# Attention outputs turned in 32x32 blocks by VectorE, with w_in's rows to match: a local-global attention followed by a hardswish MLP

## The chip, the cores and the metric

The kernel runs on one core of one Trainium2 chip. The metric is device time in microseconds; three runs of the kernel before the change have a median of 340.51 us (339.76 to 341.34).

## The reference

Eight batches of attention with 8 heads of 64. Each batch has 512 local tokens, which attend to a band of 32 tokens to each side and to the 32 global tokens, and 32 global tokens, which attend to everything. All 4352 rows then pass an MLP of 512 to 2048 to 512 with a hardswish between.

```python
s_g = scale * np.matmul(q_g, k_all.transpose(0, 1, 3, 2))
out_g = np.matmul(sm(s_g), v_all)
s_ll = np.where(np.abs(pos[:, None] - pos[None, :]) <= 32, scale * np.matmul(q_l, k_l.transpose(0, 1, 3, 2)), -1e9)
s_l = np.concatenate([scale * np.matmul(q_l, k_g.transpose(0, 1, 3, 2)), s_ll], axis=-1)
out_l = np.matmul(sm(s_l), np.concatenate([v_g, v_l], axis=2))
x = np.concatenate([out_g, out_l], axis=2).transpose(0, 2, 1, 3).reshape(B * S, H * D)
h = x @ w_in
return (h * np.clip(h + 3.0, 0.0, 6.0) / 6.0) @ w_out
```

## The kernel before

Everything runs in fp16 with fp32 sums. A planner (`Plan`) writes one static order for all engines: operations stand in named streams, each with engine, cost, dependencies and the buffers that it takes, and `lay` picks, again and again, the operation that can start first, ranked by stream among those that start at nearly the same time. Low ranks go first. `SWITCH` is what the planner charges PE for going between tile shapes, `ALONE` and `SPARE` are its thresholds for a single group of small tiles and for giving an eviction to VectorE (DVE) rather than ScalarE (ACT).

Attention of a batch has four local pairs (`local`, two 32-token blocks from each half of the batch) and two global groups (`globe`, four heads each). A pair goes through these stages:

- `s`: products of q and k in small tiles into PSUM banks `s` (batch 0 partly into `m`), 64 matmuls in batches 0 and 1 and 32 later;
- `mx`: DVE adds the mask and takes the maximum, eight times (line 664); `ex`: ACT exponentiates, eight times (line 670);
- `t`: eight PE transposes into bank `t` (line 679); `etc`: the result is copied to SBUF as `et`, by ACT or DVE (lines 308 and 310, the helper `either`);
- `av`: 32 PE matmuls with V into the banks `a` (line 693); `nm`: DVE takes reciprocals and multiplies (lines 701 and 702), which gives `x`, 128 x 512 in fp16;
- `xp`: four PE transposes of 128 x 128 through bank `t` (line 715); `xpc`: a copy to `xt` by ACT or DVE.

The two global groups do the same with maxima over two banks, `top` (lines 751 and 752), five transposes (line 768), products with V of their own (line 777), normals (lines 785 and 786), and one transpose for both at the end (line 792), which fills `xg`.

The MLP's first half (`first`, line 821) takes `xt` against `w_in` for 16 units `c` of 128 hidden columns, four matmuls each, into one of three banks `m`; ACT makes the clipped part `t1` (line 833) and DVE the product `gts` (the gate, line 828). Batch 0 is done in two halves of 256 tokens, the other batches in one of 512. The second half (`second`, line 850) takes `gts` against `w_out`, 16 matmuls of 512 columns for a tile of 128 rows, copies the sum to `ot` (lines 858 and 860), and SP's queue stores it. The global rows of all batches go through the MLP together at the end (`moe_global`), and one last local tile after them is done in two column halves. The planner lays MLP work of earlier batches between the attention of later ones.

All DMAs are issued at line 298: loads with a cast to fp16 on POOL's queue, on SP's queue the stores and the copies inside SBUF (`rawq`, `rawk`, `gn`, `vs` from `vg`). q and k of batches 2 to 7 are turned by DVE in 32 x 32 blocks (lines 571, 575, 578). POOL also shifts V into strips (line 486).

`xt` holds hidden row d of heads in an order that `load_w_in` matches, since its DMAs put the rows of `w_in` in the same order on the 128 partitions.

## Time and profile before

| | |
|---|---|
| median of three runs | 340.51 us (339.76 to 341.34) |
| the profiled execution's own time | 340.96 us |
| its span on the core | 339.2 us |
| PE, DVE, ACT busy | 313.6, 257.0, 234.1 us |
| mean granted clock of PE | 0.983 |
| instructions on PE (matmuls), DVE, ACT, POOL | 4456, 952, 576, 195 |

The span runs from the first to the last instruction in the trace; the execution's own time has what lies around it as well. The profile's groups name line, engine, operation, output and input, count, busy time, mean time of one and the idle time before them with what ended it. Its timeline gives start and length of runs of equal instructions. PE's lengths include the time that a matmul spends in the array, so that neighbours overlap.

### The profile page before, as it was taken

The numbers are of one execution on the slowest core, as the hardware profiler recorded it, in microseconds if no ns is written. First come the engines' busy times: TensorE is split into PE (matmuls) and PEld (weight loads), VectorE is DVE, ScalarE is ACT, GpSimd is POOL, SyncE is SP. The second block draws the span as 40 slices with busy tenths as digits, with TensorE's granted clock in tenths as the row PEclk, the third lists the DMA queues.
The fourth block names the chain that finished last, engine by engine and source line by source line (L and its number), as shares of the span: only waits on it lengthen the run. The fifth ranks groups of instructions, "written<-read, shape, count | busy, mean of one in ns | idle before, by whom it ended". The sixth has DMA issues, their size and how long they took to land.

```text
span 339.2 us, 11248 instructions
## 1 busy us (share of the span) xinstructions
PE 313.6 (92%) x4456; PEld 169.5 (50%) x4456; DVE 257.0 (76%) x952; ACT 234.1 (69%) x576; POOL 156.2 (46%) x195
## 2 busy tenths in 40 slices
PE   0648879899999999999999999999999999999996
PEld 0536656454455455544554555454545544445654
DVE  5887997678988799989998999899969844433310
ACT  4778778555888697679867784799699644443431
POOL 8899589108961982694359258756000000000000
PEclk9976999999999999999999999999999999999999
DMA  8989999979960996999679948991000000010103
GB/s 131 185 154 165 185 227 164 177 204 147 221 124 35 154 206 86 91 153 179 145 99 150 169 90 80 183 174 41 31 33 34 35 32 33 31 60 34 62 34 92
DMA packets 107076, 39.27 MB, mean 116 GB/s; under 512 B 92368, under 2 KB 100816, under 8 KB 107024
## 3 DMA queue, kind: packets, MB, share of 16 engines
q0 software_dynamic: 93536, 17.44, 64.6%
q1 hardware_dynamic: 12912, 20.99, 22.7%
q8 instruction: 35, 0.57, 0.7%
q10 hardware_dynamic: 576, 0.13, 0.2%
q14 instruction: 17, 0.14, 0.1%
HBM read 35.39 MB, written 8.91 MB: 131 GB/s over the span
## 4 chain that ended last, share of the span: by engine, by line
PE 87%; DVE 7%; issue 2%; POOL 1%; ACT 1%; POOLq 0%; ACTq 0%
PE m L850 36%; PE m L821 33%; PE t L679 5%; PE a L693 3%; PE s L624 2%; PE t L715 2%; DVE gts L828 1%; PE t L768 1%; PE s L735 1%; PE s L637 1%; PE a L777 1%; DVE sm L664 1%; POOL wout L298 1%; DVE kt L534 1%; DVE qt L529 1%
## 5 line engine op out<-in xcount | busy, mean ns | idle before, releaser
L850 PE MATMUL m<-wout,gts 128*128 128x512 f16 (+1 forms) x560 | 135.1, 373 | 0.0
L828 DVE SCALAR_TENSOR_TENSOR gts<-t,m 128x512 f16<-128x512 f32 (+1 forms) x160 | 95.2, 602 | 46.1 <-ACT t L833 45.0
L821 PE MATMUL m<-xt,win 128*128 128x512 f16 (+1 forms) x576 | 126.9, 359 | 3.0 <-DVE gts L828 1.9
L833 ACT ACTIVATE t<-m 128x512 f32<-128x512 f32 (+1 forms) x160 | 84.3, 532 | 44.6 <-PE m L821 41.2
L486 POOL COPY vs<-v 32x1056 f32<-32x1056 f32 (+3 forms) x81 | 78.2, 966 | 34.9 <-DMA v<-in_v_l_dram 30.1
L670 ACT ACTIVATE ex<-sm,mx 128x128 f16<-128x128 f32 x256 | 86.1, 394 | 8.4 <-DVE mx L664 7.9
L821 PEld LDWEIGHTS <-win 128*128 128x128 f16 x640 | 59.9, 99 | 54.3 <-issue 4.2
L850 PEld LDWEIGHTS <-gts 128*128 128x128 f16 x560 | 51.1, 98 | 48.5 <-issue 0.7
L664 DVE CUSTOM_DVE_ANT_0 sm<-s,mask 128x128 f32<-128x128 f32 x240 | 56.9, 285 | 5.9 <-PE s L624 2.9
L858 ACT COPY ot<-m 128x512 f32<-128x512 f32 (+1 forms) x34 | 19.5, 573 | 16.9 <-PE m L850 16.2
L298 POOL DMA_DIRECT2D rawq<-in_q_l_dram x12 | 12.6, 1057 | 36.2 <-DMA vs<-vg 16.3
L298 POOL DMA_DIRECT2D v<-in_v_l_dram x32 | 28.2, 905 | 0.0
L702 DVE TENSOR_TENSOR x<-a,rec 128x512 f16<-128x512 f32 x32 | 22.1, 692 | 1.1
L664 DVE DVE_READ_ACCUMULATOR2_ANT mx<- 128x1 f32 x256 | 21.3, 83 | 0.0
L679 PE MATMUL t<-ident,ex 128*128 128x128 f16 x256 | 20.9, 228 | 0.0
L679 PEld LDWEIGHTS <-ex 128*128 128x128 f16 x256 | 17.2, 102 | 5.5 <-issue 0.7
L637 PE MATMUL s<-kt,qt 32*32 32x128 f16 x384 | 7.0, 246 | 12.3 <-DVE kt L542 10.0
L571 DVE STREAM_TRANSPOSE qt<-rawq 128x512 f16<-128x512 f16 x24 | 15.9, 692 | 0.0
L575 DVE STREAM_TRANSPOSE kt<-rawk 128x512 f16<-128x512 f16 x24 | 15.8, 687 | 0.0
L308 ACT COPY et<-t 128x1024 f16<-128x1024 f16 x13 | 13.1, 1010 | 3.5 <-PE t L679 3.4
L637 PEld LDWEIGHTS <-qt 32*32 32x32 f16 x512 | 6.5, 102 | 17.7 <-issue 9.6
L310 DVE COPY et<-t 128x1024 f16<-128x1024 f16 x19 | 13.0, 685 | 3.0 <-PE a L693 2.6
(95 smaller groups left out, 262.7 us busy)
## 6 DMA issues: line engine op xcount, KB each, us to landing
out_dram<-ot SPq DMA_DIRECT2D x31, 256.0 KB, 2.1
vs<-vg SPq DMA_DIRECT2D x32, 132.0 KB, 5.8
v<-in_v_l_dram POOLq DMA_DIRECT2D x32, 128.0 KB, 6.5
rawq<-in_q_l_dram POOLq DMA_DIRECT2D x12, 256.0 KB, 5.8
rawk<-in_k_l_dram POOLq DMA_DIRECT2D x12, 256.0 KB, 7.2
rawq<-rawq SPq DMA_DIRECT2D x12, 254.0 KB, 5.6
rawk<-rawk SPq DMA_DIRECT2D x12, 254.0 KB, 5.7
win<-in_moe_w_in_dram POOLq DMA_DIRECT2D x8, 256.0 KB, 6.2
```

The lines of the kernel that those rows point to most:

```text
L298: eng.dma_start(out=o() if callable(o) else o, in_=i() if callable(i) else i)
L486: (nc.gpsimd if op.engine == "POOL" else nc.vector).tensor_copy(out=o(), in_=i())
L637: nc.tensor.matmul(out=scored(r)[quarter(e ^ r, f), z:z + P], lhsT=pairs(qt[k.slot])[rows, c, i * W:(i + 1) * W, bb], rhs=pairs(kt[k.slot] ...
L664: nc.vector.tensor_tensor_reduce(out=sms[sm.slot], in0=scored(c // 2)[:, z:z + P], in1=masks[:, m, :], scale=-scale, scalar=3.0e38, op0=AL ...
L670: nc.scalar.activation(out=exs[ex.slot][:, un, c, :], in_=sms[sm.slot], func=EXP, scale=-1.0, bias=mxs[mx.slot])
L679: nc.tensor.matmul(out=turned(tp)[:, z:z + P], lhsT=exs[ex.slot][:, un, c, :], rhs=ident, is_transpose=True)
L702: nc.vector.tensor_tensor(out=xs[x.slot], in0=o[:, :, :, 0:D], in1=recs[rec.slot].to_broadcast([P, 2, NC, D]), op=ALU.mult)
L821: nc.tensor.matmul(out=o if len(x.shape) == 2 else o.rearrange("p (a c) -> p a c", a=2), lhsT=w_in_t[c // 8][:, m, (c % 8) * P:(c % 8 + 1) ...
L828: nc.vector.scalar_tensor_tensor(out=g, in0=shape(t1s[t1.slot][:, 0:n]), scalar=1.0, in1=shape(mps[ps.slot][:, 0:n]), op0=ALU.min, op1=ALU ...
L833: r = plan.add("t1", Op(("ACT", 0.09 + n * 0.00083), lambda: nc.scalar.activation(out=t1s[t1.slot][:, 0:n], in_=mps[ps.slot][:, 0:n], func ...
L850: nc.tensor.matmul(out=mps[ps.slot][:, 0:n], lhsT=gfn(c), rhs=w_out_t[c // 4][:, c % 4, cols], start=(c == 0), stop=(c == NDFF - 1))
L858: nc.scalar.copy(out=o, in_=i)
```

## The change

- The four PE transposes of `x` and their copy become one DVE transpose in 32 x 32 blocks from `x` straight to `xt`; those of the global outputs likewise, straight to `xg`. A block transpose moves no data between groups of 32 partitions, so the products with V now write each head to the group of partitions that it needs (`values`), and `w_in`'s rows are loaded in the new order, over 128 partitions in place of 64.
- Tokens lie in `xt` in another order, so each tile of 128 result rows is stored in two halves of 64 rows.
- The two global groups of a batch are joined from their products with V on: `globe` computes scores to `et`, and the new `globe_values` does both groups' products, one normal and one block transpose. Their two score banks are one tile, and one instruction takes the maximum over both.
- In batch 0 and in `moe_global`, two units `c` share a bank `m`, one clipped part and one gate of 512 columns. The buffers `gts` are held in groups of four units (`CG`).
- The planner's ranks and two of its thresholds have other values, so its order differs everywhere.

```diff
-    SWITCH, ALONE = 0.097, 0.0
-    SPARE, PHASES = 0.3, 9
+    SWITCH, ALONE = 0.097, 0.5
+    SPARE, PHASES = 0.6, 9
...
+    PARTS, CG = 2, 4
...
-    for c in range(NDFF):
+    for c in range(NDFF // CG):
...
-    gts = [tiles(f"gts{r}_", NDFF, [P, Sl], FP16) for r in range(2)]
+    gts = [tiles(f"gts{r}_", NDFF // CG, [P, CG, Sl], FP16) for r in range(2)]
...
-    sps = tiles("s", 2, [P, 512], FP32, pp)
+    sps = tiles("s", 1, [P, 2, 512], FP32, pp)[0]
...
-                       ("s", -1), ("mx", lambda n: 1.2 if n < 33 else 2.7), ("ex", 1.2), ("t", -0.5), ("etc", 0), ("av", 0), ("nm", 0),
-                       ("xp", -1.2), ("xpc", 0), ("gx", 1), ("gxc", 1),
-                       ("mf", lambda n: 9 + n * 1e-3), ("ms", lambda n: 9 + (n + 2 * NDFF + 2) * 1e-3), ("t1", 0), ("gate", -1.4), ("ot", 1.5)):
+                       ("s", -1), ("mx", lambda n: 1.2 if n < 33 else 2.7), ("ex", 1.2), ("t", -0.5), ("etc", 0), ("av", -1.5), ("nm", 0),
+                       ("xp", -0.5), ("gx", 1),
+                       ("mf", lambda n: 9 + n * 1e-3), ("ms", lambda n: 9 + (n + PARTS * NDFF + 2) * 1e-3), ("t1", 0.7), ("gate", 0.1), ("ot", 2.2)):
...
-        rows = moe_w_in.rearrange("(k a e d) c -> a k d e c", k=2, a=2, e=2)
+        rows = moe_w_in.rearrange("(k h a d) c -> k a h d c", k=2, h=4, a=2)
         got = []
         for i in range(2):
             for k in range(2):
                 for a in range(2):
-                    got.append(load("l0", "POOL", 0.65, 1.4, w_in_t[i][a * D:(a + 1) * D, 2 * k:2 * k + 2],
-                                    rows[a, k, :, :, i * n:(i + 1) * n], got[-AHEAD:][:1] if len(got) >= AHEAD else ()))
+                    got.append(load("l0", "POOL", 0.65, 1.4, w_in_t[i][:, 2 * k + a], rows[k, a, :, :, i * n:(i + 1) * n],
+                                    got[-AHEAD:][:1] if len(got) >= AHEAD else ()))
...
         def values():
             o = summed(av)
             for un, i in enumerate(pair):
-                for c in range(NC):
-                    for e in range(2):
-                        for f in range(2):
-                            nc.tensor.matmul(out=o[quarter(e, f), un, c, 0:D + 1],
+                for f in range(2):
+                    for kh in range(2):
+                        for hq in range(4):
+                            h = 4 * kh + hq
+                            c, e = h // 2, h % 2
+                            nc.tensor.matmul(out=o[hq * W:(hq + 1) * W, f, 2 * un + kh, 0:D + 1],
                                              lhsT=ets[et.slot][:, un, c, quarter(e, f) if b >= WORDS else quarter(e ^ (c // 2), f)],
-                                             rhs=vs[v.slot][:, i % NU, (i + NI * f) // NU, 2 * c + e, 0:D + 1])
+                                             rhs=vs[v.slot][:, i % NU, (i + NI * f) // NU, h, 0:D + 1])
...
-        xt, xp = st["xt"], Buf(home, 1)
+        xt = st["xt"]
 
         def xturn():
-            o = turned(xp)[:, 0:4 * P].rearrange("d (k z n q) -> d k z n q", k=2, z=NU, n=2)
-            for un in range(2):
-                for kk in range(2):
-                    nc.tensor.matmul(out=o[:, kk, :, un, :], lhsT=xs[x.slot][:, un, 2 * kk:2 * kk + 2].rearrange("p a d -> p (a d)"),
-                                     rhs=ident, is_transpose=True)
-        a = plan.add("xp", Op(("PE", 0.24), xturn, done, [xp], [x], lat=0.25, n=8))
-        st["xT", n] = either(
-            "xpc", 0.5, 0.36,
-            lambda: xts[xt.slot].rearrange("d k (f t) -> d k f t", f=2)[:, :, :, 2 * n * W:(2 * n + 2) * W],
-            lambda: turned(xp)[:, 0:4 * P].rearrange("d (k f t) -> d k f t", k=KC, f=2), [a], new, [xp])
+
+            nc.vector.transpose(out=xts[xt.slot][:, :, n * P:(n + 1) * P].rearrange("p k (t q) -> p t k q", q=W),
+                                in_=xs[x.slot].rearrange("p f (u k) (a q) -> p (f u) (k a) q", u=2, a=2))
+        st["xT", n] = plan.add("xp", Op(("DVE", 0.7), xturn, done, new, [x]))
...
         def top():
-            for f in range(2):
-                nc.vector.tensor_reduce(out=tops[mx.slot][:, f:f + 1], in_=sps[f][:, 0:N1].rearrange("q (a c) -> q a c", a=1), axis=AX, op=ALU.max)
-            nc.vector.tensor_scalar(out=mxs[mx.slot], in0=tops[mx.slot][:, 0:1], scalar1=tops[mx.slot][:, 1:2], scalar2=-scale,
-                                    op0=ALU.max, op1=ALU.mult)
-        t = plan.add("mx", Op(("DVE", 1.0), top, [sc], [mx], ()))
+            nc.vector.tensor_reduce(out=tops[mx.slot][:, 0:1], in_=sps[:, :, 0:N1], axis=AX, op=ALU.max)
+            nc.vector.tensor_scalar(out=mxs[mx.slot], in0=tops[mx.slot][:, 0:1], scalar1=-scale, scalar2=None, op0=ALU.mult)
+        t = plan.add("mx", Op(("DVE", 0.86), top, [sc], [mx], ()))
...
-        def values():
+        def values(av):
             for i in range(NJ + 1):
                 val = v0[v.slot][:, i] if i < NJ else vg[v.slot]
                 for cc, e, z in four:
-                    nc.tensor.matmul(out=aps[av.slot][z, 0, 0:D + 1], lhsT=etgs[et.slot][:, i * P + z.start:i * P + z.stop],
-                                     rhs=val[:, 2 * (2 * cc + s) + e, 0:D + 1], start=(i == 0), stop=(i == NJ))
-        a = plan.add("av", Op(("PE", 0.26), values, [c, st["g4"]] + st["v0"], [av], [et, v], lat=0.3, n=40, mode=("tall", "tall")))
-        if s == 0:
-            st["xgn"] = Buf("xgn", 1)
-        xgn, rec = st["xgn"], Buf("rec", 1)
+                    q = 2 * of(cc) + e
+                    nc.tensor.matmul(out=aps[av.slot][q * W:(q + 1) * W, 0, cc * D1:cc * D1 + D + 1],
+                                     lhsT=etgs[et.slot][:, i * P + z.start:i * P + z.stop],
+                                     rhs=val[:, 4 * cc + q, 0:D + 1], start=(i == 0), stop=(i == NJ))
+        st.setdefault("globe", []).append((values, c, et))
+
+    def globe_values(b):
+
+        st = state[b]
+        both, v = st["globe"], st["v"]
+        av, xgn, rec = Buf("a", 1), Buf("xgn", 1), Buf("rec", 1)
+        a = plan.add("av", Op(("PE", 0.48), lambda: [f(av) for f, _, _ in both], [c for _, c, _ in both] + [st["g4"]] + st["v0"],
+                              [av], [et for _, _, et in both] + [v], lat=0.3, n=80, mode=("tall", "tall")))
 
         def normal():
-            nc.vector.reciprocal(out=recs[rec.slot][:, 0, 0, :], in_=aps[av.slot][:, 0, D:D + 1])
-            nc.vector.tensor_tensor(out=xgns[xgn.slot][:, s, :], in0=aps[av.slot][:, 0, 0:D],
-                                    in1=recs[rec.slot][:, 0, 0, :].to_broadcast([P, D]), op=ALU.mult)
-        n = plan.add("nm", Op(("DVE", 0.36), normal, [a], [rec] + ([xgn] if s == 0 else []), [av, rec]))
-        st.setdefault("gn", []).append(n)
-        if s == 1:
-            tp2 = Buf(home, 1)
-            a = plan.add("gx", Op(("PE", 0.06), lambda: nc.tensor.matmul(
-                out=turned(tp2)[:, 0:P], lhsT=xgns[xgn.slot].rearrange("q s d -> q (s d)"), rhs=ident,
-                is_transpose=True), st["gn"], [tp2], [xgn], lat=0.25, n=2))
-            st["xg"] = either("gxc", 0.25, 0.2, lambda: xg[:, :, b * Sg:(b + 1) * Sg],
-                              lambda: turned(tp2)[:, 0:P].rearrange("d (k g) -> d k g", k=KC), [a], (), [tp2])
+            o = aps[av.slot][:, 0, 0:2 * D1].rearrange("p (k d) -> p k d", k=2)
+            r = recs[rec.slot][:, 0, 0:2, :]
+            nc.vector.reciprocal(out=r, in_=o[:, :, D:D + 1])
+            nc.vector.tensor_tensor(out=xgns[xgn.slot], in0=o[:, :, 0:D], in1=r.to_broadcast([P, 2, D]), op=ALU.mult)
+        n = plan.add("nm", Op(("DVE", 0.45), normal, [a], [rec, xgn], [av, rec]))
+        st["xg"] = plan.add("gx", Op(("DVE", 0.22), lambda: nc.vector.transpose(
+            out=xg[:, :, b * Sg:(b + 1) * Sg], in_=xgns[xgn.slot].rearrange("p k (a q) -> p (k a) q", q=W)), [n], (), [xgn]))
...
-    def first(xfn, n, gfn, deps, takes, reads):
+    def first(xfn, n, cs, gfn, deps, takes, reads):
+
         ps, t1 = Buf("m", 1), Buf("t1", 1)
-        two = lambda t: t if len(t.shape) == 2 else t.rearrange("p a c -> p (a c)")
-
-        def mm(c):
+        all_ = n * len(cs)
+
+        def mm(k, c):
             for m in range(KC):
                 x = xfn(m)
-                o = mps[ps.slot][:, 0:n]
-                nc.tensor.matmul(out=o if len(x.shape) == 2 else o.rearrange("p (a c) -> p a c", a=2),
+                nc.tensor.matmul(out=mps[ps.slot][:, k * n:(k + 1) * n],
                                  lhsT=w_in_t[c // 8][:, m, (c % 8) * P:(c % 8 + 1) * P], rhs=x,
                                  start=(m == 0), stop=(m == KC - 1))
 
...
-        def make(c):
-            a = paced(Op(("PE", 4 * n * 0.000423), lambda: mm(c), deps + w_in_l[c // 8], [ps], reads, lat=0.25, n=8), n / Sl / NDFF)
-            r = plan.add("t1", Op(("ACT", 0.09 + n * 0.00083), lambda: nc.scalar.activation(
-                out=t1s[t1.slot][:, 0:n], in_=mps[ps.slot][:, 0:n], func=RELU, bias=0.5, scale=1.0 / 6.0), [a], [t1], ()))
-            return plan.add("gate", Op(("DVE", 0.07 + n * 0.00104), gate, [r], takes, [ps, t1]))
-        return make
+        a = [paced(Op(("PE", 4 * n * 0.000423 + (0.02 if n < 256 else 0.0)), lambda k=k, c=c: mm(k, c), deps + w_in_l[c // 8], [] if k else [ps], reads, lat=0.25, n=8), n / Sl / NDFF)
+             for k, c in enumerate(cs)]
+        r = plan.add("t1", Op(("ACT", 0.09 + all_ * 0.00083), lambda: nc.scalar.activation(
+            out=t1s[t1.slot][:, 0:all_], in_=mps[ps.slot][:, 0:all_], func=RELU, bias=0.5, scale=1.0 / 6.0), a, [t1], ()))
+        return plan.add("gate", Op(("DVE", 0.2 + all_ * 0.00078), gate, [r], takes, [ps, t1]))
...
-        st["gts"] = [Buf(f"gts{c}", NJ) for c in range(NDFF)]
+        st["gts"] = [Buf(f"gts{c}", CG * NJ) for c in range(NDFF // CG)]
         st["gd"] = {c: [] for c in range(NDFF)}
-        parts = 2 if b == 0 else 1
+        parts = PARTS if b == 0 else 1
         n = HB // parts
+        per = NI // 2 // parts
...
+            for c in range(0, NDFF, parts):
+                cs = range(c, c + parts)
+                g = st["gts"][c // CG]
+
...
+                got = first(lambda m, view=view: view(xts[xt.slot][:, m, :]) if parts > 1 else xts[xt.slot][:, m, :], 2 * n, cs, gated,
+                            deps, [g] if at == 0 and c % CG == 0 else [], [xt])
+                for d in cs:
+                    st["gd"][d].append(got)
 
     def moe_second(b, j, parts=1):
         st = state[b]
-        row = b * S + Sg + j * P
-        second(lambda c: gts[st["gts"][c].slot][c][:, j * P:(j + 1) * P], lambda c: [st["gts"][c]], lambda c: st["gd"][c],
-               [(out[row:row + P, :], 0, P)], parts)
+        rows = out[b * S + Sg:(b + 1) * S].rearrange("(f r) d -> f r d", f=2)
+        second(lambda c: gts[st["gts"][c // CG].slot][c // CG][:, c % CG, j * P:(j + 1) * P], lambda c: [st["gts"][c // CG]], lambda c: st["gd"][c],
+               [(rows[f, j * P // 2:(j + 1) * P // 2], f * P // 2, P // 2) for f in range(2)], parts)
 
...
             for s in range(2):
                 globe(b, s)
+            globe_values(b)
```

51 lines of the change are left out of this document (27 added, 24 removed).

## The prediction

> **What bounds the kernel now.** I read the page first (engine shares, the chain that ended last), then busy time by stretches.
>
> ```profile
> PE 313.6 (92%) x4456; PEld 169.5 (50%) x4456; DVE 257.0 (76%) x952; ACT 234.1 (69%) x576; POOL 156.2 (46%) x195
> PE 87%; DVE 7%; issue 2%; POOL 1%; ACT 1%; POOLq 0%; ACTq 0%
> ...
> 21.00:22.00 1.00, 0.18 (x15) 0.02 (x3) 0.73 (x2) 0.26 (x1) 0.96 (x3) 0.50 0.46 83
> ...
> 28.00:30.00 2.00, 2.00 (x11) 1.39 (x10) 0.61 (x2) 1.62 (x4) 2.00 (x4) 0.50 0.97 167
> ...
> 31.00:32.00 1.00, 1.00 (x12) 0.66 (x8) 0.88 (x3) 0.85 (x3) 1.00 (x3) 1.00 1.09 175
> ...
> 120.00:140.00 20.00, 20.00 (x280) 10.31 (x279) 19.77 (x75) 16.14 (x42) 9.33 (x11) 1.00 0.80 111
> ...
> 70.00:327.00 257.00, 256.96 (x3296) 130.91 (x3295) 201.94 (x715) 181.43 (x422) 103.95 (x111) 1.00 0.78 102
> ```
>
> In the stretches the columns are length, then PE, PEld, DVE, ACT and POOL busy, PE's granted clock, DMA share, GB/s. From 70 to 327 us PE is busy 256.96 of 257: there an instruction taken from PE shortens the end by its own time, as long as nothing new makes PE wait. DVE is the runner-up, 19.77 of 20 in the worst stretch, so what the change gives to DVE is the danger. Before 70 us PE waits, and from 21 to 30 us it runs at a granted clock of 0.50.
>
> What PE pays for each kind of group is read from the starts in its timeline (start, then length; a length overlaps the next group, so starts count):
>
> ```profile
> 78.70 0.22 PE L792 MATMUL t<-ident,xgn 128*128 128x128 f16 x1
> 78.75 1.03 PE L821 MATMUL m<-xt,win 128*128 128x512 f16 x4
> ...
> 98.76 0.39 PE L715 MATMUL t<-ident,x 128*128 128x128 f16 x4
> 99.07 0.43 PE L693 MATMUL a<-vs,et 128*32 128x65 f16 x32
> 99.43 0.42 PE L624 MATMUL s<-kt,qt 64*32 64x128 f16 x32
> 99.78 1.04 PE L850 MATMUL m<-wout,gts 128*128 128x512 f16 x4
> 100.65 0.39 PE L715 MATMUL t<-ident,x 128*128 128x128 f16 x4
> 100.88 1.89 PE L850 MATMUL m<-wout,gts 128*128 128x512 f16 x8
> 102.70 0.43 PE L735 MATMUL s<-kt,qg 64*32 64x288 f16 x8
> ```
>
> Four transposes of an output x take 0.23 us before whole-array products (100.65 to 100.88) and 0.31 before products with V (98.76 to 99.07). The 0.08 is the price of going from whole-array matmuls to small tiles: 8 matmuls of w_out take 1.82 us (100.88 to 102.70) where four take 0.87 (99.78 to 100.65), so 0.08 again. Going back costs nothing visible: 0.36 and 0.35 for V and score groups whatever follows. The transpose of global outputs costs 0.05.
>
> **The change, part by part.** Counts of the changed program are from its built order of instructions.
>
> *PE.* 136 of 4456 matmuls go: 32 groups of four x transposes, 8 of xgn. 32 × 0.23 = 7.4, 8 × 0.05 = 0.4. With the other ranks, the order enters small tiles from whole-array work 61 times, not 76: 15 × 0.08 = 1.2. Together 9.0 us off PE. Joining the two global V groups moves no matmul.
>
> *VectorE and ScalarE.* These groups, split by shape, price what comes and goes (count, busy us, mean ns):
>
> ```profile
> L828 DVE SCALAR_TENSOR_TENSOR gts<-t,m 128x512 f16<-128x512 f32 x112 | 76.2, 682 | 30.4 <-ACT t L833 29.5
> L833 ACT ACTIVATE t<-m 128x512 f32<-128x512 f32 x112 | 66.6, 595 | 30.3 <-PE m L821 27.7 <-PE t L715 0.8 <-DVE gts L828 0.7
> L828 DVE SCALAR_TENSOR_TENSOR gts<-t,m 128x256 f16<-128x256 f32 x48 | 19.0, 416 | 15.8 <-ACT t L833 15.4
> L833 ACT ACTIVATE t<-m 128x256 f32<-128x256 f32 x48 | 17.7, 384 | 14.3 <-PE m L821 13.6 <-DVE xgn L786 0.2
> L571 DVE STREAM_TRANSPOSE qt<-rawq 128x512 f16<-128x512 f16 x24 | 15.9, 692 | 0.0
> L308 ACT COPY et<-t 128x1024 f16<-128x1024 f16 x13 | 13.1, 1010 | 3.5 <-PE t L679 3.4
> L310 DVE COPY et<-t 128x1024 f16<-128x1024 f16 x19 | 13.0, 685 | 3.0 <-PE a L693 2.6 <-PE t L679 0.2
> L751 DVE TENSOR_REDUCE top<-s 128x1 f32<-128x288 f32 x32 | 12.9, 445 | 0.9 <-PE s L735 0.9
> L308 ACT COPY xt<-t 128x512 f16<-128x512 f16 x19 | 11.1, 582 | 6.2 <-PE t L715 6.1
> L310 DVE COPY xt<-t 128x512 f16<-128x512 f16 x11 | 4.6, 423 | 3.0 <-PE t L715 2.9
> L786 DVE TENSOR_TENSOR xgn<-a,rec 128x64 f16<-128x64 f32 x16 | 3.6, 225 | 0.6
> L578 DVE STREAM_TRANSPOSE qg<-gn 128x128 f16<-128x128 f16 x6 | 1.7, 284 | 0.0
> ```
>
> DVE gains 32 transposes of the size in row L571, 32 × 0.69 = 22.1, and 8 of the size in row L578, 2.3. It loses all 19 evictions of et, which the new order gives to ScalarE (13.0), the 11 of xt (4.6), 48 half gates for 24 full ones (48 × 0.416 − 24 × 0.682 = 3.6), and half of the global maxima and normals: 16 reduces of twice the length for 32, bounded between one short reduce and two, so a gain of 0 to 16 × 0.445 = 7.1; I take 2, by the slope of rows L571 and L578 (0.41 us for 384 columns). The same way 8 longer normals for 16 give 0 to 1.8, taken as 1. Net: about nothing to DVE's load (24.4 against 24.2). ACT: +19 × 1.01 for et (18 and one from an m bank), −21 × 0.58 for xt, −(48 × 0.384 − 24 × 0.595) = −4.2 for the gates' first half, so +3. Its 181 of 257 us leaves room. Neither total becomes the bound.
>
> The Trainium skill ("VectorE: DVE Perf Modes", section The three transpose paths) gives 311 ns for a 128×128 block on VectorE and a rules table sending whole 128×128 transposes to TensorE. The 284 ns of row L578 agrees with the figure; four of them would make 1.24 us for one x and DVE's load 18 us heavier, but row L571 has 0.69 for four blocks in one instruction, and the row decides.
>
> *Order of the chain.* Before, x went DVE, PE, copy, PE:
>
> ```profile
> 25.68 0.69 DVE L702 TENSOR_TENSOR x<-a,rec 128x512 f16<-128x512 f32 x1
> ...
> 26.42 0.61 PE L715 MATMUL m<-ident,x 128*128 128x128 f16 x4 [1.21 <-DVE x L702]
> ...
> 27.14 0.56 ACT L308 COPY xt<-m 128x512 f16<-128x512 f16 x1
> ...
> 27.75 2.72 PE L821 MATMUL m<-xt,win 128*128 128x256 f16 x12
> ```
>
> From x's end (26.37) to the first w_in product 1.38 us; with a DVE transpose 0.69 + about 0.1. Each batch thus has its xT 0.6 us sooner if DVE is free. In the start that is a gain of 0 to 1.2 (two pairs), but gates in twos wait for 8 matmuls, not 4, at half clock, and then each holds DVE longer: 0 to −1.5. I take nothing, ±1.5. Later, a bank now holds two units of batch 0, so three banks cover twice the time behind DVE's long transposes; that pays for the eight x transposes that now stand in DVE's row before batch 2. By 84.9 us, where batch 2's scores start, PE now has 55 us of work behind it; in the new order 61, since all w_in products of batch 1 come ahead of it. I expect that start near 90 us, with the rest shorter by 14.
>
> *A new wait.* Walking the new order with these durations, PE runs dry once, at the end of batch 2's attention. Its list there is scores of the second global group, last V group, five transposes, then w_in products of batch 2 itself, which need the last x transposed; all w_out work of batch 1 is used up. The link from V to x:
>
> ```profile
> 70.82 0.43 PE L693 MATMUL a<-vs,et 128*32 128x65 f16 x32
> 71.18 1.04 PE L850 MATMUL m<-wout,gts 128*128 128x512 f16 x4
> ...
> 71.34 0.21 DVE L701 RECIPROCAL rec<-a 128x8 f32<-128x8 f32 x1 [0.69 <-PE a L693]
> 71.58 0.69 DVE L702 TENSOR_TENSOR x<-a,rec 128x512 f16<-128x512 f32 x1
> ```
>
> V's group gives way at 71.18, x ends at 72.27: 1.1 us. In DVE's new row a global maximum stands next (0.445 to 0.89, and its scaling), then the transpose 0.69: 2.8 us against 0.3 of transposes on PE. I take 2.5 us. Behind the waiting product on PE stand the second global transposes, the joined V group and batch 3's scores; DVE and ACT then stand idle for want of scores. In batches 1 and 3 to 7 the list has 8 to 12 w_out products (1.7 to 2.6 us) plus five or ten transposes there: cover 2.3 to 3.2 for a chain of 1.9 (no maximum between) or 2.8. Nothing lost, little to spare. After it, gates bunched between q and k transposes cost PE about 0.5.
>
> *Stores and w_in loads.*
>
> ```profile
> out_dram<-ot SPq DMA_DIRECT2D x31, 256.0 KB, 2.1
> win<-in_moe_w_in_dram POOLq DMA_DIRECT2D x8, 256.0 KB, 6.2
> L298 SPq DMA_DIRECT2D out_dram<-ot x41: 314/338/428, 61.2 to 336.5; - x41
> ```
>
> 33 local row tiles are stored in two halves: 33 more issues of 0.34 us on SP's queue, 11 us over 270, in which it mostly waits for copies. Queued behind them are the q, k and vg copies inside SBUF; each comes 0.34 later, and without the stores' own waits being earlier that would reach DVE's transposes. At the very end one more issue stands after the last copy: +0.34, less at most that much for the smaller transfer; taken as +0.3. w_in loads keep size and number; over 128 partitions the row goes up or down by at most a few tenths of the 6.2, covered by the first eight units' products. POOL's row sends some later v loads ahead of q and k; a whole batch's attention hides that. The score banks, now one tile, let the next scores begin only when all eight maxima of the last are taken; before, the second half waited for that eight small matmuls later, so nothing changes.
>
> Sum: −9.0 + 2.5 + 0.5 + 0.3 = −5.7 on the profiled span 339.2, so 333.5. That execution took 340.96 with what lies around the span, 0.45 above the median of 340.51. On the median: 334.8.
>
> **Rivals.**
>
> *No new wait* (20%): DVE's maximum slips or PE arrives late anyway, and the start gains its 1.2: 340.5 − 9.0 − 1.2 + 0.3 = 330.6. For it: the banks' better cover; against: the lists leave PE nothing else.
>
> *The clock falls at the new wait* (17%).
>
> ```profile
> 20.07 0.54 PE L637 MATMUL m<-kt,qt 32*32 32x128 f16 x41 [2.97 <-issue]
> ```
>
> PE idled from 17.1 to 20.07 us here, and the clock was 0.50 from 21 until about 31: ten us at half speed cost 5. If 2.5 us idle does the same: 334.8 + 5 = 339.8, no change to be measured. For it: that gap was only 0.5 longer; against: PE is saturated on both sides of the new one. The Trainium skill ("TensorE: Matmul & The Clock Gate", Part 1) puts the idle needed at about a 3.4 us window, by which the clock holds; the 2.97 us of this trace already was enough.
>
> *Slower* (15%): DVE answers late at the end of every batch. Its row holds gates and q/k transposes of 0.65 us, and it is 19.77 of 20 busy in one stretch. If it is late by d at the last x of each batch, PE loses 2.5 + d in batch 2, d − 0.4 in batches 1 and 4 to 7, d − 0.1 in batch 3: 0.4 + 7d in all. It eats the 9.0 from d = 1.2 us, two instructions; with three (1.9) it costs 13.7: 340.5 − 9.0 + 13.7 + 0.8 = 346. For it: w_in's products now hang on DVE's row alone, where ScalarE made most copies of xt (19 in row L308); against: DVE's load does not grow.
>
> *Not what it says* (3%): PE's transposes were hidden and nothing changes, 340.5. The 257 us stretch speaks against it.
>
> **How the numbers follow.** The forecast has 45% (332 to 337), the rivals the rest. Predicted: 334.8. Range 329 to 342: the low end is the first rival and 1.5 for the start, the high end takes in the clock; outside remain most of the slower case and a little below. What this kernel's measurement can tell from no change is 0.5%, 1.7 us. Faster: 45 + 20 and 6 of the clock's 17 (a shorter cold stretch) = 71%; same: 11 + 3 = 14%; slower: 15%.
>
> **What would show it.** PE near 4320 matmuls and about 9 us less work; DVE's share nearly as before; x's transposes near 690 ns; first 64-row scores of batch 2 near 90 us; one idle time of 2 to 3 us before a w_in product near 110 us, clock 1.00 after it. I am wrong if PE waits for xt at several batch ends, if PE's rows show 0.50 after 35 us, or if DVE's transposes take over 0.8 us.

## The result, and the profile after

| | before | after | ratio, 95% interval |
|---|---|---|---|
| median of 19 and 19 runs | 340.83 us (339.23 to 342.04) | 338.18 us (335.63 to 340.56) | 0.9918 (0.9900 to 0.9935) |
| the profiled execution's own time, its span | 340.96, 339.2 | 338.04, 336.0 | |
| forecast | | 334.8, or 0.9832 of 340.51 | |

The change makes the kernel 0.8% faster where 1.7% was forecast: the direction and most of the steps held, the size was half. The times after also spread over 4.9 us where those before spread over 2.8; part of the explanation lies there. Ratios here and below leave out the runs in the slower of the two states that executions show: one run of the version with the last x's transpose moved, three of the version with sixteen loads.

The page of the changed kernel, busy time by engine:

```profile
PE 304.3 (91%) x4320; PEld 161.9 (48%) x4320; DVE 253.4 (75%) x901; ACT 238.6 (71%) x548; POOL 156.5 (47%) x194
```

Its groups (mean ns of one behind the busy time):

```profile
L309 ACT COPY et<-t 128x1024 f16<-128x1024 f16 x31 | 31.3, 1009 | 4.3 <-PE t L680 4.3
L717 DVE STREAM_TRANSPOSE xt<-x 128x512 f16<-128x512 f16 x32 | 22.5, 703 | 0.1
...
L749 DVE TENSOR_REDUCE top<-s 128x1 f32<-128x576 f32 x16 | 12.0, 747 | 1.7 <-PE s L734 1.5 <-PE s L742 0.2
```

PE has 9.3 us less work, with 4320 matmuls. The x transposes are on VectorE at 0.703 us each, and its load falls by 3.6 us, not by nothing. ScalarE gains 4.5.

The span is 3.2 us shorter. PE's timeline says where, at three marks. First, the start (idle time before a row in brackets, with what ended it):

```profile
12.91 0.72 PE L638 MATMUL s<-kt,qt 32*32 32x128 f16 x20 [1.92 <-DVE mx L665]
15.20 1.05 PE L638 MATMUL s<-kt,qt 32*32 32x128 f16 x64 [0.39 <-DVE mx L665]
21.41 0.79 PE L638 MATMUL m<-kt,qt 32*32 32x128 f16 x41 [3.74 <-issue]
25.45 0.68 PE L742 MATMUL s<-kt,qg 32*32 32x288 f16 x16 [1.72 <-DVE mx L665]
28.81 1.01 PE L820 MATMUL m<-xt,win 128*128 128x256 f16 x4 [1.77 <-DVE xt L717]
```

The first w_in product starts at 28.81, before at 27.75: 1.06 us lost. Scores now wait for maxima ("<-DVE mx") at three places, where the first of them waited 1.32 us for k before:

```profile
12.32 0.97 PE L637 MATMUL s<-kt,qt 32*32 32x128 f16 x20 [1.32 <-DVE kt L534]
```

The stall marked "<-issue" is 3.74 us where it was 2.97. The profile shows nothing that PE waits for in such a stall; that it waits for its instructions is a reading.

Behind the first product the half clock also lasts longer. These are the stretches in which it ends (the column behind the five engines is the granted clock), before and after:

```profile
30.00:31.00 1.00, 1.00 (x36) 0.51 (x34) 0.42 (x1) 0.82 (x4) 1.00 (x2) 0.53 0.97 171
```

```profile
34.00:35.00 1.00, 1.00 (x33) 0.57 (x35) 0.59 (x1) 0.28 (x2) 0.35 (x1) 0.69 1.28 184
```

So PE runs at half clock for 3.2 us behind the first product before, and for 5.8 after: by estimate another 1.3 us lost, in this execution.

Second, the end of batch 2's attention:

```profile
111.58 0.42 PE L697 MATMUL a<-vs,et 128*32 128x65 f16 x32
111.93 0.45 PE L765 MATMUL t<-ident,eg 128*128 128x128 f16 x5
114.57 1.02 PE L820 MATMUL m<-xt,win 128*128 128x512 f16 x4 [2.18 <-DVE xt L717]
115.43 0.44 PE L765 MATMUL t<-ident,eg 128*128 128x128 f16 x5
115.70 1.89 PE L820 MATMUL m<-xt,win 128*128 128x512 f16 x8
117.52 0.31 PE L775 MATMUL a<-v,etg 128*32 128x65 f16 x16
```

That is the forecast's new wait, at its place, 2.18 us long, and the only idle time of PE from 68 us to the end.

Third, the tail, in the timeline of all engines, before:

```profile
326.34 9.70 PE L850 MATMUL m<-wout,gts 128*128 128x512 f16 x60
...
336.07 0.37 ACT L858 COPY ot<-m 128x256 f32<-128x256 f32 x1 [1.33 <-PE m L850]
```

and after:

```profile
324.76 6.03 PE L847 MATMUL m<-wout,gts 128*128 128x512 f16 x43
324.90 8.72 SPq L299 DMA_DIRECT2D out_dram<-ot  x11
...
330.83 0.37 ACT L855 COPY ot<-m 128x256 f32<-128x256 f32 x1 [1.37 <-PE m L847]
```

The last product ends at 336.04 before and 330.79 after. From there to the end of the span it is 3.16 us before and 5.21 after. So between the first w_in product and the last product PE needs 308.29 and 301.98 us: 6.31 less, with the longer half clock already in it. The balance: +1.06 − 6.31 + 2.05 = −3.2.

Why the tail is longer shows in the waits of SP's queue from 325 us on (total, times, longest); before:

```profile
SPq L298 <- ACT ot L858: 6.5, 3, 3.9
```

and after:

```profile
SPq L299 <- ACT ot L855: 1.6, 1, 1.6
```

Before, SP waited for the copies. After, it is itself late: the copies of ot end at 331.20, the last store is issued until 333.62 (324.90 + 8.72). Some of the issues have become longer as well; the tile view of ot has their least, median and greatest ns, for the last ten before:

```profile
L298 SPq DMA_DIRECT2D out_dram<-ot x10: 314/412/428, 329.7 to 336.5; - x10
```

and for the last seven after (the five ahead of them took 0.31 to 0.43 us, as before):

```profile
L299 SPq DMA_DIRECT2D out_dram<-ot x7: 421/547/1827, 328.3 to 333.0; - x7
```

Twelve stores follow the last global products now, ten before (the last local tile in four pieces, not two), and one issue took 1.83 us.

The theory tested first: the loss against the forecast lies in the start, from the score banks as one tile (S) and w_in's loads over 128 partitions (W). Rivals: PE's transposes were worth less than 0.23 us a group; the clock falls at the new wait in executions that were not profiled; the gates in twos. The tail comes last.

### The profile page after: what moved, and what is told of

Its sections match the earlier page's. It is cut to its first block, busy times and chain, and to the rows that moved or that the text cites. A ratio compares the mean times of both kernels' runs of the same rounds, so it can differ in the third digit from the quotient of the medians.

```text
span 336.0 us, 10857 instructions
## 1 busy us (share of the span) xinstructions
PE 304.3 (91%) x4320; PEld 161.9 (48%) x4320; DVE 253.4 (75%) x901; ACT 238.6 (71%) x548; POOL 156.5 (47%) x194
## 4 chain that ended last, share of the span: by engine, by line
PE 84%; DVE 9%; issue 3%; ACT 2%; POOL 1%; ACTq 0%; POOLq 0%; DVEq 0%
PE m L820 34%; PE m L847 34%; PE t L680 4%; PE a L697 3%; PE s L625 3%; PE s L638 1%; DVE sm L665 1%; PE t L765 1%; DVE x L706 1%; DVE xt L717 1%; PE s L734 1%; DVE gts L827 1%; POOL wout L299 1%; DVE qt L530 1%; DVE kt L535 1%
## 5 line engine op out<-in xcount | busy, mean ns | idle before, releaser
L847 PE MATMUL m<-wout,gts 128*128 128x512 f16 (+1 forms) x560 | 131.0, 374 | 0.0
L820 PE MATMUL m<-xt,win 128*128 128x512 f16 (+1 forms) x576 | 121.7, 361 | 6.0 <-DVE xt L717 4.0
L827 DVE SCALAR_TENSOR_TENSOR gts<-t,m 128x512 f16<-128x512 f32 x136 | 91.5, 681 | 36.4 <-ACT t L831 35.7
L831 ACT ACTIVATE t<-m 128x512 f32<-128x512 f32 x136 | 80.5, 596 | 37.7 <-PE m L820 36.6
L820 PEld LDWEIGHTS <-win 128*128 128x128 f16 x640 | 61.8, 100 | 61.4 <-issue 8.4
L671 ACT ACTIVATE ex<-sm,mx 128x128 f16<-128x128 f32 x256 | 84.3, 394 | 4.7 <-DVE mx L665 4.0
L309 ACT COPY et<-t 128x1024 f16<-128x1024 f16 x31 | 31.3, 1009 | 4.3 <-PE t L680 4.3
L717 DVE STREAM_TRANSPOSE xt<-x 128x512 f16<-128x512 f16 x32 | 22.5, 703 | 0.1
L697 PEld LDWEIGHTS <-et 128*32 128x32 f16 x1024 | 10.2, 98 | 13.4 <-ACT ex L671 4.9
L299 POOL DMA_DIRECT2D rawk<-in_k_l_dram x12 | 12.5, 1045 | 8.3 <-DVE kt L576 7.7
## 6 DMA issues: line engine op xcount, KB each, us to landing
win<-in_moe_w_in_dram POOLq DMA_DIRECT2D x8, 256.0 KB, 10.5
```

Source lines behind the costliest of these rows:

```text
L299: eng.dma_start(out=o() if callable(o) else o, in_=i() if callable(i) else i)
L309: nc.scalar.copy(out=o(), in_=i())
L671: nc.scalar.activation(out=exs[ex.slot][:, un, c, :], in_=sms[sm.slot], func=EXP, scale=-1.0, bias=mxs[mx.slot])
L717: nc.vector.transpose(out=xts[xt.slot][:, :, n * P:(n + 1) * P].rearrange("p k (t q) -> p t k q", q=W), in_=xs[x.slot].rearrange("p f (u k ...
L820: nc.tensor.matmul(out=mps[ps.slot][:, k * n:(k + 1) * n], lhsT=w_in_t[c // 8][:, m, (c % 8) * P:(c % 8 + 1) * P], rhs=x, start=(m == 0), ...
L827: nc.vector.scalar_tensor_tensor(out=g, in0=shape(t1s[t1.slot][:, 0:all_]), scalar=1.0, in1=shape(mps[ps.slot][:, 0:all_]), op0=ALU.min, o ...
```

## The experiments

Ratios are to the kernel before on the same chip.

### The start: one score tile and w_in's loads

*Two score tiles in the changed kernel (S undone).*

```diff
-    sps = tiles("s", 1, [P, 2, 512], FP32, pp)[0]
+    sps = tiles("s", 2, [P, 512], FP32, pp)
...
-            nc.vector.tensor_reduce(out=tops[mx.slot][:, 0:1], in_=sps[:, :, 0:N1], axis=AX, op=ALU.max)
+            for f in range(2):
+                nc.vector.tensor_reduce(out=tops[mx.slot][:, f:f + 1], in_=sps[f][:, 0:N1].rearrange("q (a c) -> q a c", a=1), axis=AX, op=ALU.max)
...
```

> The changed kernel with the two score banks as two tiles again (and two maxima for each global group as before, about 0.14 us more on DVE each); the order of everything else is kept. Theory S: in the changed kernel's start, scores wait for maxima of the other bank, since both banks are one tile (idle 1.92, 0.39, 1.72 and 0.47 us on PE that end with the maxima); with two tiles these waits go and the scores of batch 2 begin 1.5 to 2.5 us earlier than at 92.8 us: median near 336.2. Theory W (the new w_in loads delay the start) and theory C (it is only the clock): no change, 338.

*The loads of the kernel before in the changed kernel (W undone).*

```diff
-        rows = moe_w_in.rearrange("(k h a d) c -> k a h d c", k=2, h=4, a=2)
+        rows = moe_w_in.rearrange("(k a e d) c -> a k d e c", k=2, a=2, e=2)
...
-                    got.append(load("l0", "POOL", 0.65, 1.4, w_in_t[i][:, 2 * k + a], rows[k, a, :, :, i * n:(i + 1) * n],
+                    got.append(load("l0", "POOL", 0.65, 1.4, w_in_t[i][a * D:(a + 1) * D, 2 * k:2 * k + 2], rows[a, k, :, :, i * n:(i + 1) * n],
```

> The changed kernel with w_in loaded over 64 partitions as before the change, so w_in's rows lie where the kernel before had them and the output is not the reference's; the order of everything else is kept. Theory W: the new loads have 384 more packets each and land after 10.5 us in place of 6.2, which holds back v (DVE's first copies of v at 18.8 us against 17.5) and the instruction fetch that PE waits for (3.7 against 3.0 us); with the old loads the scores of batch 2 begin 1 to 2 us earlier and the median falls to 336.5. Theory S: no change, 338.

*Both undone.*

> Both of the above: two score tiles and w_in over 64 partitions, output not the reference's. If S and W are both right and add up: 334.5 to 335, the forecast's number, with batch 2's scores near 90 us. If only one is right: as that one alone.

*One score tile alone, in the kernel before.*

> The kernel before with its two score banks made one tile, nothing else. Theory S: PE's waits for maxima appear in the start of the kernel before too, and it gets 1 to 2 us slower: 342. Theories W and C: no change, 340.8.

| | time | ratio, 95% interval |
|---|---|---|
| S undone | 337.94 | 0.9911 (0.9879 to 0.9943) |
| W undone | 337.29 | 0.9886 (0.9850 to 0.9922) |
| both undone | 335.81 | 0.9858 (0.9830 to 0.9886) |
| S alone, in the kernel before | 341.15 | 1.0008 (0.9987 to 1.0029) |

Both together give back 0.6% (2.0 us), either alone nothing that its interval separates from the changed kernel's 0.9918, and one tile alone costs the kernel before nothing that its interval shows. What each does is in the rows. With S undone the first scores wait as before the change:

```profile
12.31 0.96 PE L638 MATMUL s<-kt,qt 32*32 32x128 f16 x20 [1.32 <-DVE kt L535]
21.43 0.79 PE L638 MATMUL m<-kt,qt 32*32 32x128 f16 x41 [4.35 <-issue]
```

but what PE gains (it has reached the stall 0.6 us earlier) the stall takes back: 4.35 us until 21.43, where it ended at 21.41 with one tile. With both undone the stall ends sooner:

```profile
20.33 0.79 PE L638 MATMUL m<-kt,qt 32*32 32x128 f16 x41 [3.24 <-issue]
...
28.02 1.01 PE L822 MATMUL m<-xt,win 128*128 128x256 f16 x4 [1.78 <-DVE xt L717]
```

What W changes is in the software queue (packets, MB, share) and in the loads' time to landing, after:

```profile
q0 software_dynamic: 96608, 17.45, 66.6%
...
win<-in_moe_w_in_dram POOLq DMA_DIRECT2D x8, 256.0 KB, 10.5
```

and with W undone:

```profile
q0 software_dynamic: 93536, 17.44, 65.1%
...
win<-in_moe_w_in_dram POOLq DMA_DIRECT2D x8, 256.0 KB, 6.5
```

Eight loads of unchanged size make 3072 more packets and land in 10.5 us instead of 6.2 before.

A microsecond at this mark in one profile proves little, though. In six of the profiles (the changed kernel and five versions that change something later) PE's start is the same instruction for instruction, and yet the first w_in product starts anywhere from 27.94 to 29.64. Leaving out the sixteen loads and the single gates below, the new order has it at 27.67 to 28.02 in three profiles with the old loads, and at 27.94 to 30.75 in nine with the new ones. Three of those nine have S undone, and are not early (28.84, 29.92, 30.75). In the kernel before, one tile alone has 29.16, and with the new loads too it is 28.07. So in the new order the rows point to W, but not firmly, and what S costs by itself is not shown.

*Both in the kernel before.*

> The kernel before, with the score banks as one tile and w_in's loads over 128 partitions as in the changed kernel, but the rest as before; rows of w_in then don't stand where x's rows expect them, so the output differs from the reference's. If the two parts by themselves cost the start what the changed kernel got back without them (338.18 to 335.81 us, 2.4), the time is about 343.0 (ratio 1.007). Rival: they cost only together with the new order of gates in twos, and here the score tile's +0.5 us is all: 341.2 (ratio 1.001).

342.63 us, ratio 1.0036 (1.0018 to 1.0055): +1.2 us, between the two expectations. The two parts do cost something by themselves, but some 60% of what undoing them gave back, and its profile has the first w_in product only 0.3 later than before (28.07 after 27.75). This is the cleaner of the two figures, since no new wait stands behind it.

*Sixteen loads of 64 partitions with the new rows*, on the version with the wait short and filled (below).

```diff
-                    got.append(load("l0", "POOL", 0.65, 1.4, w_in_t[i][:, 2 * k + a], rows[k, a, :, :, i * n:(i + 1) * n],
+                    for g in range(2):
+                        got.append(load("l0", "POOL", 0.325, 0.7, w_in_t[i][g * D:(g + 1) * D, 2 * k + a], rows[k, a, g, :, :, i * n:(i + 1) * n],
...
```

> The version with the wait short and filled, and w_in loaded in 16 transfers over 64 partitions each (128 KB, the rows that x's new layout needs) instead of 8 over 128: eight more issues on POOL's queue. If it is the number of partitions of a load that makes 384 more packets and the longer landing, the software queue has about 93,500 packets again, a load lands in under 6.5 us, and the time falls by 0.5 to 1 us below that version's. Rival: the packets come from the row groups of 32 (96,600 packets stay), and eight more issues of 0.6 us on POOL cost the start 0.5 to 2 us.

Ratio 1.0032 (1.0005 to 1.0058), 100,832 packets in the software queue. The planner also laid out another order, and the output is not the reference's, for a reason that stays open, so nothing is concluded from the time. But the packets rose instead of falling, and the loads, of half the size, still took 9.8 us to land: it is not the number of partitions alone that makes the packets.

*Gates of batch 0 singly.*

```diff
-            for c in range(0, NDFF, parts):
-                cs = range(c, c + parts)
+            for c in range(NDFF):
+                cs = range(c, c + 1)
...
```

> The changed kernel with the gates of batch 0 one unit at a time (48 more and shorter instructions on ScalarE and VectorE against 24 fewer long ones, three banks for one unit each), as in the kernel before. If gates in twos cost the start by making the first gates wait for eight products at half clock, batch 2's first scores come 1 to 1.5 us earlier than 92.8 and the time is near 336.9 (ratio 0.988). Rival: the banks cover less behind VectorE's long transposes, and the time is 339 to 340 (ratio 0.995 to 0.998). The forecast took the two as equal: 0.992.

339.92 us, ratio 0.9948 (0.9921 to 0.9974). Gates in twos are not what the start lost: without them it is a microsecond worse, as the rival had it (the two intervals still overlap a little), although in this order 12 w_out products stand where the new wait was, and that wait is gone. PE waits for gates at 45.39 (1.51 us) and 48.45 (1.59) where the changed kernel has one such wait of 1.35.

### What PE's transposes are worth

*The x transposes twice, in the kernel before.*

```diff
-                    nc.tensor.matmul(out=o[:, kk, :, un, :], lhsT=xs[x.slot][:, un, 2 * kk:2 * kk + 2].rearrange("p a d -> p (a d)"),
-                                     rhs=ident, is_transpose=True)
+                    for _ in range(2):
+                        nc.tensor.matmul(out=o[:, kk, :, un, :], lhsT=xs[x.slot][:, un, 2 * kk:2 * kk + 2].rearrange("p a d -> p (a d)"),
+                                         rhs=ident, is_transpose=True)
```

> The kernel before, with every transpose of an output x done twice on PE (the second writes the same values to the same place): 128 more matmuls, in 32 groups of four, the order of groups kept. If PE's transposes stood on the path at 0.23 us for a group, as the forecast took, the time rises by 32 x 0.23 = 7.4 us, to about 348.1 (ratio 1.022). Rival: they were hidden in part by waits in the start and at batch ends, so that taking them away could not give 7.4; then the rise is 4 us or less (ratio at most 1.012).

348.93 us, ratio 1.0233 (1.0214 to 1.0252): +7.9 us for 32 groups, 0.25 each. The forecast's largest term, 7.4, was right, as far as adding four transposes shows what taking four away is worth, and the rival is out.

### The end of batch 2

*The last x's transpose ahead of the maximum.*

```diff
+        move("xp", 11, "mx", 101)
```

> The changed kernel, with one instruction moved: on DVE, the transpose of batch 2's last x stands before the second global maximum instead of behind it and its scaling. If the new wait of 2.18 us is the chain V, x, maximum, transpose, it becomes 1.3 to 1.4 us and the time falls by 0.8, to a ratio near 0.9895 against the kernel before. Rival: the later maximum delays the exponentials and transposes of the second global group, PE waits there instead, and the time stays (ratio 0.992).

336.45 us, ratio 0.9877 (0.9850 to 0.9905); the interval just touches the changed kernel's. The wait is 1.45 us, as expected, but the rows behind it are new:

```profile
113.27 1.02 PE L820 MATMUL m<-xt,win 128*128 128x512 f16 x4 [1.45 <-DVE xt L717]
114.64 0.86 PE L765 MATMUL t<-ident,eg 128*128 128x128 f16 x5 [0.35 <-ACT eg L754]
115.29 3.31 PE L820 MATMUL m<-xt,win 128*128 128x512 f16 x8
```

Eight products in 3.31 us: half speed. The same stands behind the new wait in the profile with both parts of the start undone; first PE's timeline, then the stretches:

```profile
113.04 1.49 PE L822 MATMUL m<-xt,win 128*128 128x512 f16 x4 [2.30 <-DVE xt L717]
114.33 0.74 PE L767 MATMUL t<-ident,eg 128*128 128x128 f16 x5
114.86 2.89 PE L822 MATMUL m<-xt,win 128*128 128x512 f16 x8
117.68 0.31 PE L777 MATMUL a<-v,etg 128*32 128x65 f16 x16
```

```profile
113.00:114.00 1.00, 0.96 (x4) 0.44 (x4) 1.00 (x2) 0.27 (x1) 0.00 (x0) 0.73 1.52 98
114.00:115.00 1.00, 1.00 (x8) 0.72 (x7) 0.77 (x2) 0.43 (x1) 0.00 (x0) 0.50 1.86 207
115.00:116.00 1.00, 1.00 (x4) 0.30 (x3) 0.80 (x2) 0.79 (x2) 0.00 (x0) 0.50 2.33 167
116.00:117.00 1.00, 1.00 (x4) 0.35 (x3) 0.51 (x1) 0.19 (x1) 0.05 (x1) 0.56 2.11 135
```

From the first product to the V group it is 4.64 us (113.04 to 117.68), in the changed kernel's own profile 2.95 (114.57 to 117.52): 1.7 us lost, in a step at half clock of about 3.4 us. Of the six profiles that have a wait of 1.4 to 2.3 us here, five show it, with 1.4 to 1.7 us lost; the changed kernel's own is the one that doesn't.

How often it happens in the runs that were not profiled can be estimated from their mean granted clock, since 3.4 us at half clock lower it by 0.005 over 336 us. Of the changed kernel's 19 runs, eleven lie at 0.978 to 0.984 or at 0.999 and 1.000, and eight about 0.005 below one of these levels, at 0.974 and 0.975 or 0.993 to 0.995. The medians of the two groups are 336.96 and 338.98 us. So the fall is a matter of the execution, and going by this mark it comes in under half of them; it is an estimate, because the record of the clock can miss a slow stretch (last section). One of the six runs with both parts of the start undone has the mark, so about 0.4 of the 2.0 us above may be the clock's.

*Shorter by four moves, and two score tiles.*

```diff
+        move("xp", 11, "mx", 101)
+        move("etc", 15, "ex", 100)
+        move("ms", 31, "av", 13, True)
...
```

> The changed kernel with the two score tiles of the kernel before (and their two reduces), and at batch 2's end four moves: the last x's transpose before the second global maximum on DVE, the copy of the last local weights before the first global exponentials on ScalarE, and the last four w_out products of batch 1 on PE (with the copy and the stores behind them) behind the last V group. If the rest of the loss is the new wait, it shrinks from 2.2 us to less than 1, and the time falls below that of two score tiles alone by 1.2 to 2: a ratio of 0.985 to 0.988. Rival: what leaves that wait comes back at the next one (batch 3's scores or DVE's row of k transposes), and the ratio stays at 0.991.

338.09 us, ratio 0.9903 (0.9872 to 0.9935), a miss. The wait for x fell to 0.58, at full clock, but 0.69 and 0.47 appeared around it where PE waits for the exponentials of the global groups: 1.74 us in all instead of 2.18, as the rival had it.

*The wait filled.* Nine products that nobody reads, in a bank that the next group overwrites.

```diff
             op.emit()
+            if op is plan.streams["t"][16]:
+                for _ in range(9):
+                    nc.tensor.matmul(out=mps[2], lhsT=ident, rhs=w_out_t[0][:, 0], start=True, stop=True)
```

> The changed kernel, and in the new wait at the end of batch 2 (behind the first five transposes of global weights) nine matmuls of 512 columns into a product bank that is free and overwritten next: 1.96 us of work that nobody reads, in a gap of 2.18. Theory: that wait lets the clock fall in most executions (profiles of three other versions show 0.50 for 3.4 us behind it, a loss of 1.4 us; the profile of the changed kernel itself doesn't); kept busy, PE stays at 1.00, the products behind it take 0.87 for four and 1.82 for eight, and the median falls by 0.7 to 1.4 us, to a ratio of 0.988 to 0.990. Rival: the clock doesn't fall there in runs that are not profiled, or work that nobody reads pushes the chain back: ratio 0.992 or more.

336.39 us, ratio 0.9861 (0.9833 to 0.9890). PE's timeline:

```profile
113.26 2.11 PE L958 MATMUL m<-wout,ident 128*128 128x512 f16 x9
115.60 1.02 PE L820 MATMUL m<-xt,win 128*128 128x512 f16 x4 [0.23 <-DVE xt L717]
```

Work that is worth nothing makes the kernel 0.57% faster (1.9 us; the two intervals together leave 0.8 to 3). The wait is as long as ever, only the clock doesn't fall: none of the five profiles with the wait filled shows half speed behind it, and one of their 28 runs has the mark. Eight falls in 19 runs at 1.7 us would be 0.7 us, so either the mark misses some falls or part of the 1.9 is not explained.

*Short and filled.* The moved transpose and six such products.

> The changed kernel with the last x's transpose of batch 2 ahead of the second global maximum (a wait of 1.45 us instead of 2.18), and that wait filled with six matmuls of 512 columns that nobody reads (1.31 us). Theory: the moved instruction gave 0.7 us and the fill gives the 1.4 us that the profile of that version lost to a clock of 0.50 behind the wait: a ratio of 0.983 to 0.986, the best with the reference's output. Rival: the wait's loss is only its own length: 0.988 as without the fill.

336.38 us, ratio 0.9862 (0.9830 to 0.9893): no better than filled alone. The profiles say why: from the five transposes to the V group PE takes 5.64 us here (111.96 to 117.60) and 5.59 with the wait filled alone (112.97 to 118.56). What the moved transpose saves comes back behind the first four products, where PE waits for the exponentials of the second global group, as the rival of that experiment had it.

### The tail, and all together

*Every second of the last twelve stores from ScalarE's queue.*

```diff
-                     [c], (), [ot])
+                     [c], (), [ot], by=nc.scalar if late and at % 2 else None)
```

> The changed kernel with every second one of the last twelve stores (the global tiles and the last local half tiles) issued from ScalarE's queue instead of SP's. Theory: SP's queue stands 1.8 us behind the last copy, so the end comes sooner by 0.7 to 1.5 us: from the end of the last copy to the end of the span 3.0 to 3.5 us instead of 4.8, a ratio of 0.988 to 0.990. Rival: the transfers themselves are what is late, or ScalarE's own issues delay the last copies: 4 us or more, and a ratio of 0.992.

337.90 us, ratio 0.9899 (0.9865 to 0.9933). In the profile the end comes 3.2 us after the last copy (333.36 to 336.6), not 4.8, and as much in the three versions below; the nine profiles of the new order with SP's queue alone range from 3.5 to 4.8, and the four of the old order have 2.7. So the queue is what is late. In the time, the gain of 0.6 us is inside the interval; five of these six runs have the mark of the fallen clock, so the time can't price the stores.

*Short, filled and two queues.*

> The changed kernel with batch 2's last transpose ahead of the maximum, six idle products in the wait, and the last twelve stores from two queues. Theory: the gain of the first two (0.9862) and that of the stores (0.002 to 0.004) add: a ratio of 0.982 to 0.985. Rival: the stores give nothing: 0.986.

336.24 us, ratio 0.9865 (0.9839 to 0.9891): the stores add nothing that can be measured, and the rival holds; there was little to gain, since the two profiles have 3.5 and 3.2 us behind the last copy.

*All three places away.*

> The changed kernel with two score tiles, the w_in loads of the kernel before (rows of w_in then don't stand where x's rows expect them, so the output differs from the reference's), nine idle products in the new wait and the last twelve stores from two queues. If the three places account for the loss, the time stands below the forecast's ratio of 0.983 (which had 0.3 for the tail and no cold clock): 0.979 to 0.983. Rival: what is taken away in one place comes back in another, and it stays at the 0.986 of the first two alone.

*The same with the changed kernel's own loads.*

> As the version with all three away, but with the changed kernel's own w_in loads, so that the output is the reference's: two score tiles, nine idle products, two store queues. If w_in's loads cost 1 us or more even so, the ratio is 0.982 to 0.986, 0.003 above the version without them; rival: equal to it within its interval, so that loads over 128 partitions cost nothing by themselves.

With all three away 335.64 us, ratio 0.9843 (0.9823 to 0.9864); with the changed kernel's own loads 336.16, 0.9853 (0.9829 to 0.9877). The first just misses its expectation of 0.979 to 0.983, and its interval takes the forecast's 0.9832 in. The medians don't add: 0.60% (start), 0.57% (fill) and 0.19% (stores), alone, would make 1.36%; together they give 0.75%. The second is the fastest version with the reference's output, 0.65% under the changed kernel; between it and the other filled versions the runs don't decide. Nor do they between the two here, so that with S and the wait away the rival stands, and no cost of the loads is shown in the medians.

What W may do there is widen the spread: four runs without it lie between 335.42 and 335.91, six with it between 334.98 and 338.97. The slowest of these was profiled, and has a second stall that the other hasn't:

```profile
28.73 0.24 PE L697 MATMUL a<-vs,et 128*32 128x65 f16 x2 [2.32 <-issue]
30.75 1.01 PE L822 MATMUL m<-xt,win 128*128 128x256 f16 x4 [1.77 <-DVE xt L717]
```

PE's stalls marked "<-issue" up to 100 us, added up, are 4.9 to 8.6 us in the nine profiles of the changed kernel's kind with one gate order and the new loads, and 5.0 to 5.8 in the three with the old ones. That w_in's packets hold up the fetching of instructions is the reading that fits, but the kernel before with both parts has 5.3, so it is not shown.

## Why the prediction was half right

- *PE's transposes, 32 × 0.23 = 7.4, and 9.0 off PE in all:* right. Doubling them costs 7.9; busy time fell by 9.3.
- *VectorE and ScalarE don't become the bound; x transposes near 690 ns:* right, 703. The price of a figure for one block times four, 1.24, is out.
- *The new wait, 2.5 us near 110 us, once, x's transpose behind a maximum:* right in place, cause and size (2.18); 301.98 against 308.29 us from the first w_in product to the last makes −6.31 where the terms −9.0 + 2.5 + 0.5 gave −6.0. That this sum agrees so well is luck in part: it holds some 1.3 us of the longer half clock behind the start, which none of the terms had, and without which it would be about −7.6.
- *"The score banks, now one tile, ... so nothing changes"* and w_in's loads *"up or down by at most a few tenths of the 6.2, covered by the first eight units' products"*, and with both *"I take nothing, ±1.5"* for the start: this is the first step that failed. The start was put at nothing, and it cost: the first w_in product came 1.06 later in the profile (within the ±1.5 that was allowed), and the half clock behind it lasted 2.6 us longer. One tile makes the first scores wait 0.6 longer, and the stall behind them took that back; the loads took 10.5 us and not 6.2. Undoing both gives 2.0 us; in the kernel before, adding both costs 1.2. How the loads hold up the start stays open. Gates in twos, suspected there with up to 1.5, were no cost: singly is slower.
- *Stores, "+0.3" at the tail:* the second step that failed, mis-sized: 2.05 in the profile and some 0.8 to 2.1 over the profiles. This is 1.75 more than forecast; with the 1.06 of the start, and 0.3 less in between, it makes up the 2.5 us by which the profiled span missed its forecast of 333.5. The last issue was counted alone; the queue behind which it stands, with twelve stores and issues of up to 1.83 us, was not.
- *The clock falls at the new wait (17%, 339.8):* the mechanism was right, but it was kept out of the sum, and its price was wrong. It shows in five of six profiles, and by the mean clock in eight of 19 runs; it costs 1.4 to 1.7 us in the profiles, not 5: the cold step lasts about 3.4 us, not ten, with PE busy right behind it. That is the third share of what is missing. The mark that the forecast gave, "clock 1.00 after it", held in the profile of the changed kernel by the luck of that execution, which by itself hides this. The Trainium skill ("TensorE: Matmul & The Clock Gate", Part 1) has windows of about 3.4 us that run freely, so that it depends on the execution where a gap falls in them; the length of the cold step agrees, while the idle window that it asks for does not: 1.45 us of wait were enough here.
- *First scores of batch 2 near 90 us:* they came at 92.82. The later start explains about one of the 2.8 us, and the longer half clock behind it, by the estimate above, another 1.3; the mark was poor as well, since the amount of w_in work ahead of it differs between two orders.

With all three places away the ratio is 0.9843, against 0.9918 and a forecast of 0.9832: together they hold most of what is missing. What stays open: how the three shares split in an execution that isn't profiled, as they don't add, why the same start takes 1.7 us longer in one execution than in another, and why single stores take over a microsecond to issue.

## What to carry to other kernels

A change that takes work from the bounding engine is worth that work where the engine is saturated, but its side edits (one tile for two banks, another shape for a load, twice the stores) are paid at the ends of the kernel, where the engine isn't: price them there, queue by queue. A short wait in a saturated stretch can cost nearly twice its length through the clock, differently in each execution (here 2.2 us, and 1.4 to 1.7 more); look at the lengths of the matmuls behind it in several profiles before calling it cheap, and fill it if it can't be removed.

## What the hardware showed that was not expected

The granted clock in the record can miss a slow stretch. With both parts of the start undone the record has 1.00 from 28 to 29 us, although four products of 256 columns take 0.80 us from start to start there (28.02 to 28.82), and 0.44 at full speed (301.15 to 301.59 in the changed kernel). The lengths are the safer witness:

```profile
28.00:29.00 1.00, 0.98 (x6) 0.73 (x6) 1.00 (x11) 0.00 (x0) 1.00 (x2) 1.00 1.04 160
```

A wait of 1.45 us was enough to let the clock fall in one profile, and one of 2.18 us was not in another; three waits of 0.47 to 0.69 within 5 us were not in the one profile that has them.
